# Four moves in the order of a two-layer kernel: a reading, a memset, a weight split and the parts of a tile

## The chip, the cores and the metric

The kernel runs on one core of a Trainium2 chip. The metric is device time in microseconds, the median of the runs shown. The profile is one further execution, recorded by the hardware profiler. The engines are called PE (TensorE, matmuls; PEld are its weight loads), DVE (VectorE), ACT (ScalarE), POOL (GpSimd) and SP (SyncE, which here only issues DMAs). Each runs its own instruction stream in a fixed order and waits on semaphores for the others.

## The reference

Four layers run over x of 2048 tokens x 640 features, in the order A, B, A, B, both A layers with the same weights and both B layers too. H is 32 heads of 20. Each layer adds its result to x.

```python
def _A_ref(x, wqkv, wo):            # x is layer-normed
    q, k, v = qkv[0], qkv[1], qkv[2]
    phi = lambda t: jnp.where(t > 0, t + 1, jnp.exp(t)) + 1e-6
    pq, pk = phi(q), phi(k)
    kv = jnp.einsum("bhsd,bhse->bhde", pk, v)
    z = jnp.einsum("bhsd->bhd", pk)
    num = jnp.einsum("bhqd,bhde->bhqe", pq, kv)
    den = jnp.einsum("bhqd,bhd->bhq", pq, z)[..., None] + 1e-6
    return (num / den) @ wo         # heads merged first
```

Layer B is causal softmax attention inside four segments of 512 tokens, mixed by a gate with a linear-attention memory that is carried from segment to segment, and a last product with its own `wo`. Only its weights and the key stacks of its attention matter here.

## The kernel before

**Staging.** A segment is 512 tokens, four tiles of 128. Matrices are split into two f16 halves, a rounded one and its rest, and a product is made of three f16 products; so 640 features are 5 blocks times 3, 15 matmuls for a tile and 320 columns ("a half").

**Layer A by algebra.** Values are never formed. Over the four segments the kernel sums G, the product of the normed x (its split form `xs`) with phi of the keys (`pk`), 640 x 640, in `g_first`: for each tile two key halves (`keys`), two query halves (`queries`, written to DRAM as `pqd`), and for each segment ten product chains of G (`memory`, L546 to L565, 12 matmuls each, summed on DVE at L562 or L564). In the first segment of the first layer all keys come first, then G, then the queries. In the last segment `merge` (L588) takes over: it sums the key column sums over all rows (L609) into `zb` and its scaled reciprocal `rz` (L610 to L612), takes the last chains of G, and forms from each block of G a "part": `eps` (L624), the scaled block `ge` (L626), its f16 copy on ACT (L628) and its rest on DVE (L629), five parts for each half of the columns. Then PE multiplies them with the value weight (L642), DVE and ACT cut the result to the heads (`kt`, L646 to L654), and PE multiplies with `wo` (L674, L679) into one matrix `wm`.

**The second half of layer A.** `p_read` (L694) reads a finished tile of queries: a DMA on SP (L698), a multiply with `zb` on POOL (L699), a sum for each head on DVE (L702), two small steps (L703, L704) and a second multiply on POOL (L705). `a_head` (L710) waits in the program for `L["zb"]`, reads three tiles and, once `wm` is there, turns the first. `a_second` (L721) reads the fourth, loads the residual rows `xo`, turns each tile (`turn`, L312: PE transposes, an ACT copy, a DVE subtraction), multiplies with `wm` (`o_half`), adds, and norms the result for layer B (`xh`).

**Weights.** `w_prep` (L228) loads a weight through the pool `stage` (two buffers), pauses `wait` pulls, takes the largest magnitude (DVE L240, L245; PE L248; DVE L250), pauses again, broadcasts it (PE L254), forms the scale, splits five blocks (ACT L264, DVE L265) and stores the split to DRAM (SP L270). With `behind` the reductions L240 are queued behind the last DVE subtraction of `turn`. `opening` (L1062) decides when each weight is prepared. Key weight first; `parts` (L475) makes `xs` from a normed tile (a copy on ACT, a subtraction on POOL).

**Side streams.** `weave(main, aux, per)` (L98) draws one piece of the main stream and then `per` pulls of the side stream; a pull is one step up to the next `yield`. In the opening's first segment `per` is 3, otherwise 2. `turns` alternates between two streams, `pause(n)` is n empty pulls. In the last segment the side stream prepares the key weight and the output weight of B and then runs `a_head`.

**The attention's pool.** `open_b` (L755) opens it in place of `stage` when the opening is over: three key stacks `ks`, whose rows 60, 61, 124 and 125 have to hold a constant. A memset fills the tile `one` (L760) and six DMAs on SP copy it (L763).

**What sets the order.** PE runs in the order in which the program writes its instructions. DVE, ACT, POOL and SP get theirs from a list scheduler that works through estimated times: of the instructions ready on an engine it takes the one written first, and a later one where none of those is ready. Instructions in a `high_priority` block go ahead of those outside. `issue_after(ins)` puts each instruction that its block writes on the engine of `ins` behind `ins` on that engine. The order is fixed before the run.

Of the kernel before, what the change touches and what calls it, by code (L numbers as in the profile page):

```python
# [14 lines left out]
OP = mybir.AluOpType  # L15
# [112 lines left out]
def pause(n):  # L128
    for _ in range(n):
        yield 0.0  # L130
# [12 lines left out]
class Kernel:  # L143
# [444 lines left out]
    def merge(self, L, wv, wo, memory, fill):  # L588
# [17 lines left out]
        for n in range(2):  # L606
# [6 lines left out]
            yield 4 * HN * COL  # L613
        L["zb"] = zb
        gs, eps = [], sb.tile([P, C], F32, tag="rca", name="eps", bufs=3)
        for n in range(2):
# [4 lines left out]
            for c in range(C):  # L621
                e = sb.tile([P, SEG], F32, tag="pq", name="ge", bufs=PQ)[:, :HN]
                if n == 0:
                    nc.vector.tensor_scalar(eps[:, c:c + 1], L["G"][c][:, HN:HN + 1], self.k_scl, 1e-6,  # L624
                                            op0=OP.mult, op1=OP.mult)
                nc.vector.scalar_tensor_tensor(e, L["G"][c][:, n * (HN + 1):n * (HN + 1) + HN], eps[:, c:c + 1],  # L626
                                               rz[:, n * HN:(n + 1) * HN], op0=OP.add, op1=OP.mult)
                nc.scalar.activation(t[:, c, 0, :HN], e, AF.Copy)  # L628
                nc.vector.tensor_tensor(t[:, c, 1, :HN], e, t[:, c, 0, :HN], op=OP.subtract)  # L629
        for _ in memory:  # L630
# [63 lines left out]
    def p_read(self, L, s, i, o):  # L694
# [3 lines left out]
        self.q_pqi.dma_start(pq, L["pqd"][s][i])  # L698
        nc.gpsimd.tensor_tensor(pq, pq, L["zb"][:, :D], op=OP.mult)  # L699
        q3 = pq.rearrange("p (h e) -> p h e", e=DH)  # L700
# [54 lines left out]
    def open_b(self):  # L755
        self.bp = self.ctx.enter_context(self.tc.tile_pool(name="attn", bufs=1))
        nc = self.nc
        self.ks = [self.bp.tile([P, 2, SEG], F16, name=f"ks{j}") for j in range(3)]
# [303 lines left out]
    def opening(self, src, stage, L, box):  # L1062
# [3 lines left out]
        def prep(key, keep=True):  # L1066
            w = self.w_tile(key) if keep else stage.tile([P, C, 2, D], F16, tag="split", name="split", bufs=1)
            if keep:
                self.w[key] = w
            yield from self.w_prep(key, stage, w, 0 if key == ("A", "k") else 3, key == ("A", "q"))  # L1070

# [39 lines left out]
        def others():  # L1111
            self.parts(first, cur[2], 0)
            for i in range(1, NT):
                xh = self.normed(*m[i - 1])
                yield from self.turn(xh, cur[1], i)
                self.parts(xh, cur[2], i)

        o = others()
        self.ones_columns()
        for s in range(NSEG):  # L1120
            nxt = []
            if s == 0:
                aux = chain(islice(o, 2), turns(o, a("q")), self.norms(src, 1, nxt, 6))
            elif s == 1:
# [149 lines left out]
```

## Time and profile before

| | |
|---|---|
| median of 3 runs | 1750.34 us (1749.05 to 1750.95) |
| the profiled execution | 1753.38 us |
| its span, first to last instruction | 1751.6 us |
| mean granted TensorE clock | 0.989 |
| instructions | 36286 |
| ACT, POOL busy | 994.8 us (57%), 541.2 us (31%) |

The span is what the profiler saw between the first and the last instruction; the time of the execution is 1.8 us longer. A row of a timeline gives start, length, engine, line, operation, output and inputs, shape and count of a group of like instructions, and in brackets how long the engine was idle before it and what ended that. The granted clock is the share of full speed that TensorE was allowed. Layer A of the first pair takes the first 300 us or so: the opening to 230, the merge to 275, then the second half, which runs on beside layer B. The second A layer sums G up to 1085 and merges up to 1128.

### The profile page before, as it was taken

How to read it: one execution, taken by the hardware profiler on the slowest of the kernel's cores; microseconds unless marked ns; L12 is line 12 of the kernel's file. 1: busy time of each engine (PE TensorE's matmuls, PEld its weight loads, DVE VectorE, ACT ScalarE, POOL GpSimd, SP SyncE). 2: the span in 40 equal slices, each digit the busy share in tenths (PEclk: the TensorE clock that was granted, in tenths of full speed). 3: DMA queues.
4: the chain of work that ended last, by engine and by line, in shares of the span. 5: the costliest groups of instructions: out<-in, count | busy, mean ns of one | idle time of the engine just before them, and what ended most of it. 6: DMA issues, size and time to landing. Idle time of an engine off the chain costs nothing.

```text
span 1751.6 us, 36286 instructions
## 1 busy us (share of the span) xinstructions
PE 1658.7 (95%) x13032; PEld 1034.7 (59%) x13032; DVE 1252.5 (72%) x3966; ACT 994.8 (57%) x1883; POOL 541.2 (31%) x1059
## 2 busy tenths in 40 slices
PE   5999988999999999999999999999999999999998
PEld 3677655564465456556656777666546545645555
DVE  7878685378787768768874465846778777878773
ACT  5666433346646655766676463333675576676673
POOL 3542131214213342333352210220422432333452
PEclk9999989999999999999999999999999999999999
DMA  5324535331321242344211303423232323323432
GB/s 212 143 83 154 207 147 204 104 118 54 98 93 58 90 133 73 106 146 133 81 54 39 114 31 121 158 97 129 66 105 83 107 77 110 102 81 111 137 107 91
DMA packets 110365, 190.89 MB, mean 109 GB/s; under 512 B 14172, under 2 KB 69596, under 8 KB 107624
## 3 DMA queue, kind: packets, MB, share of 16 engines
q1 hardware_dynamic: 97704, 142.68, 24.8%
q0 software_dynamic: 3264, 24.91, 4.0%
q10 hardware_dynamic: 9216, 20.98, 3.1%
q8 instruction: 103, 1.69, 0.4%
q14 instruction: 78, 0.64, 0.1%
HBM read 109.32 MB, written 78.64 MB: 107 GB/s over the span
## 4 chain that ended last, share of the span: by engine, by line
PE 71%; DVE 12%; ACT 7%; DMA 4%; POOL 3%; issue 2%; SPq 1%; ACTq 0%; POOLq 0%; DVEq 0%
PE ps L395 30%; PE ps L381 13%; PE ps L988 7%; PE ps L557 4%; PE ps L961 4%; PE ps L920 3%; PE ps L319 3%; ACT pe L965 3%; PE ps L446 2%; DVE ps L926 2%; PE ps L805 2%; PE ps L1001 1%; DMA pqi<-pqd 1%; DVE split L265 1%; DMA stage<-in_B_wo 1%
## 5 line engine op out<-in xcount | busy, mean ns | idle before, releaser
L926 DVE CUSTOM_DVE_ANT_0 ps<-ps,maskw 128x384 f32<-128x384 f32 (+3 forms) x1024 | 472.7, 518 | 41.3 <-PE ps L920 38.6
L965 ACT ACTIVATE pe<-ps,lsc 128x512 f32<-128x512 f32 x640 | 395.8, 697 | 76.1 <-PE ps L961 74.8
L395 PEld LDWEIGHTS <-xT 128*128 128x128 f16 x2880 | 283.4, 99 | 119.2 <-issue 9.8
L972 POOL TENSOR_SCALAR_AFFINE_SELECT pe<-pe 128x256 f32<-128x256 f32 (+1 forms) x640 | 229.6, 366 | 371.0 <-ACT pe L965 364.2
L395 PEld LDWEIGHTS <-oT 128*128 128x128 f16 x1920 | 186.4, 99 | 85.0 <-issue 5.9
L988 PE MATMUL ps<-pe,v 128*32 128x512 f32 (+3 forms) x2048 | 164.3, 436 | 12.5 <-POOL pe L972 7.2
L395 PE MATMUL ps<-w_Ak,xT 128*128 128x320 f16 x960 | 144.0, 307 | 3.7 <-DVE w_Ak L265 2.2
L395 PE MATMUL ps<-wm,oT 128*128 128x320 f16 x960 | 144.2, 303 | 3.2 <-ACT oT L323 1.6
L395 PE MATMUL ps<-w_Bo,oT 128*128 128x320 f16 x960 | 142.8, 301 | 1.6 <-ACT oT L323 0.7
L381 PE MATMUL ps<-xT,w_Bq 128*128 128x512 f16 x600 | 140.3, 379 | 2.8 <-ACT r L419 1.6
L926 DVE DVE_READ_ACCUMULATOR2_ANT mg<- 128x1 f32 x1024 | 142.7, 139 | 0.0
L395 PE MATMUL ps<-w_Bv,xT 128*128 128x320 f16 x960 | 141.1, 301 | 1.2 <-DVE otok L1008 1.2
L381 PE MATMUL ps<-xT,w_Bk 128*128 128x512 f16 x600 | 139.7, 382 | 1.2 <-ACT pe L965 1.2
L395 PE MATMUL ps<-w_Aq,xT 128*128 128x320 f16 x960 | 139.6, 302 | 1.1 <-DVE xT L324 1.0
L557 PE MATMUL ps<-pk,xs 128*128 128x321 f16 (+1 forms) x960 | 137.4, 300 | 2.3 <-DVE pk L531 1.8
L920 PE MATMUL ps<-ks,qs 60*128 60x512 f16 (+3 forms) x1024 | 123.2, 298 | 6.8 <-ACT pe L965 3.1
L557 PEld LDWEIGHTS <-xs 128*128 128x128 f16 x960 | 93.0, 97 | 39.8 <-issue 3.9
L770 DVE SCALAR_TENSOR_TENSOR nat<-ps,nat 128x512 f16<-128x512 f32 x80 | 55.1, 689 | 82.4 <-ACT nat L769 82.2
L988 PEld LDWEIGHTS ps<-pe,v 128*32 128x32 f32 x2048 | 65.4, 109 | 74.4 <-issue 39.6
L961 PE MATMUL ps<-qs,ks 62*128 62x512 f16 (+3 forms) x1024 | 106.6, 300 | 2.3 <-ACT pe L965 1.1
L410 DVE SCALAR_TENSOR_TENSOR e<-e,r 128x320 f32<-128x320 f32 x128 | 64.7, 505 | 56.5 <-ACT r L409 55.6
L769 ACT ACTIVATE nat<-ps 128x512 f16<-128x512 f32 x80 | 48.3, 604 | 88.3 <-PE ps L381 72.0
(197 smaller groups left out, 2424.3 us busy)
## 6 DMA issues: line engine op xcount, KB each, us to landing
x<-xn ACTq DMA_DIRECT2D x48, 320.0 KB
qs<-qd SPq DMA_DIRECT2D x128, 120.0 KB
ks<-kd SPq DMA_DIRECT2D x128, 120.0 KB
xo<-x SPq DMA_DIRECT2D x48, 320.0 KB
pqi<-pqd SPq DMA_DIRECT2D x32, 320.0 KB
qd<-nat SPq DMA_DIRECT2D x40, 256.0 KB
kd<-nat SPq DMA_DIRECT2D x40, 256.0 KB
x<-in_A_x SPq DMA_DIRECT2D x16, 320.0 KB
```

The costliest lines, as they stand in the source:

```text
L319: nc.tensor.transpose(pt[:, (c - c0) * P:(c - c0 + 1) * P], src[:, c * P:(c + 1) * P], self.ident)
L381: nc.tensor.matmul(p, w[:, c, a, t * P:(t + 1) * P], xT[:, c, b, :], start=k == 0, stop=k == 3 * C - 1)
L395: nc.tensor.matmul(p, xT[:, c, a, i * P:(i + 1) * P], w[:, c, b, n * HN:(n + 1) * HN], start=k == 0, stop=k == 3 * C - 1)
L410: nc.vector.scalar_tensor_tensor(e, e, 1.0, r, op0=OP.min, op1=OP.add)
L557: nc.tensor.matmul(p, xs[:, i, a, c * P:(c + 1) * P], pk[i][:, b, cols], start=k == 0, stop=k == 3 * NT - 1)
L770: nc.vector.scalar_tensor_tensor(nat[:, 1], p, QK_SHIFT, nat[:, 0], op0=OP.mult, op1=OP.subtract)
L920: nc.tensor.matmul(bs[par][:, a:a + n], qs[r, p, i * P:(i + 1) * P], ks[r, p, :n], start=True, stop=True)
L926: nc.vector.tensor_tensor_reduce(bs[par][:, a:a + n], bs[par][:, a:a + n], self.maskw[:, SEG - n:], 1.0, NEG, OP.add, OP.max, G["mg"][:, p ...
L961: nc.tensor.matmul(b[:, a:a + n], ks[r, p, j * P:(j + 1) * P], qs[r, p, j * P:], start=True, stop=True)
L965: nc.scalar.activation(e, b, AF.Exp, scale=self.lsc)
L972: nc.gpsimd.affine_select(d, d, pattern=pat, compare_op=OP.is_ge, fill=0.0, base=0, channel_multiplier=-1)
L988: nc.tensor.matmul(G["pv"][32 * h4:32 * h4 + 32, j * P:], v[j][:, h * E1:h * E1 + 32], G.pop((p, par, j)), start=j == 0, stop=j == 2, skip ...
```

## The change

Four moves. In `merge`, `L["zb"]` is set behind both halves of the parts of G instead of ahead of them, so that `a_head` writes its readings later, and the last part's DVE subtraction is kept as `L["split"]`; in `p_read` the first multiply is put in an `issue_after` block that names it. The memset of `one` and the six DMAs move to `open_stacks`, called with high priority. The pauses of `w_prep` become 0 for the query weight of A (3 before) and 6 for the output weight of B (3 before). In the first segment the side stream turns the three remaining tiles first, makes the parts of all four behind them, and then pulls the query weight's preparation: three pulls, 14 empty ones, the rest, and then the next segment's norms; before, the parts stood between the turns, and the preparation alternated with the turns.

```diff
--- before.py
+++ after.py
@@ -611,7 +611,6 @@
             nc.vector.reciprocal(rz[:, c], zb[:, c])
             nc.vector.tensor_scalar(rz[:, c], rz[:, c], self.k_inv, G_ONE, op0=OP.mult, op1=OP.mult)
             yield 4 * HN * COL
-        L["zb"] = zb
         gs, eps = [], sb.tile([P, C], F32, tag="rca", name="eps", bufs=3)
         for n in range(2):
             for _ in range(C - 2 if n == 0 else C):
@@ -626,7 +625,8 @@
                 nc.vector.scalar_tensor_tensor(e, L["G"][c][:, n * (HN + 1):n * (HN + 1) + HN], eps[:, c:c + 1],
                                                rz[:, n * HN:(n + 1) * HN], op0=OP.add, op1=OP.mult)
                 nc.scalar.activation(t[:, c, 0, :HN], e, AF.Copy)
-                nc.vector.tensor_tensor(t[:, c, 1, :HN], e, t[:, c, 0, :HN], op=OP.subtract)
+                L["split"] = nc.vector.tensor_tensor(t[:, c, 1, :HN], e, t[:, c, 0, :HN], op=OP.subtract)
+        L["zb"] = zb
         for _ in memory:
             pass
         yield from filled(1)
@@ -696,7 +696,8 @@
         nc = self.nc
         pq = self.row("pqi")
         self.q_pqi.dma_start(pq, L["pqd"][s][i])
-        nc.gpsimd.tensor_tensor(pq, pq, L["zb"][:, :D], op=OP.mult)
+        with self.tc.issue_after(L["split"].ins):
+            nc.gpsimd.tensor_tensor(pq, pq, L["zb"][:, :D], op=OP.mult)
         q3 = pq.rearrange("p (h e) -> p h e", e=DH)
         rc = self.sb.tile([P, H], F32, tag="rca", name="rca", bufs=3)
         nc.vector.tensor_reduce(rc, q3, axis=AX.X, op=OP.add)
@@ -754,6 +755,10 @@
 
     def open_b(self):
         self.bp = self.ctx.enter_context(self.tc.tile_pool(name="attn", bufs=1))
+        with self.tc.high_priority():
+            self.open_stacks()
+
+    def open_stacks(self):
         nc = self.nc
         self.ks = [self.bp.tile([P, 2, SEG], F16, name=f"ks{j}") for j in range(3)]
         one = self.bp.tile([P, 2, SEG], F16, tag="nat", name="one", bufs=2)
@@ -1067,7 +1072,8 @@
             w = self.w_tile(key) if keep else stage.tile([P, C, 2, D], F16, tag="split", name="split", bufs=1)
             if keep:
                 self.w[key] = w
-            yield from self.w_prep(key, stage, w, 0 if key == ("A", "k") else 3, key == ("A", "q"))
+            yield from self.w_prep(key, stage, w, 0 if key[0] == "A" and keep else 6 if key == ("B", "o") else 3,
+                                   key == ("A", "q"))
 
         def a(n):
             if n not in preps:
@@ -1109,18 +1115,20 @@
         with self.tc.issue_after(self.last.ins):
             m += [self.moments(x[i]) for i in range(2, NT)]
         def others():
-            self.parts(first, cur[2], 0)
+            xh = [first]
             for i in range(1, NT):
-                xh = self.normed(*m[i - 1])
-                yield from self.turn(xh, cur[1], i)
-                self.parts(xh, cur[2], i)
+                xh.append(self.normed(*m[i - 1]))
+                yield from self.turn(xh[i], cur[1], i)
+            for i in range(NT):
+                self.parts(xh[i], cur[2], i)
 
         o = others()
         self.ones_columns()
         for s in range(NSEG):
             nxt = []
             if s == 0:
-                aux = chain(islice(o, 2), turns(o, a("q")), self.norms(src, 1, nxt, 6))
+                q = a("q")
+                aux = chain(o, islice(q, 3), pause(14), q, self.norms(src, 1, nxt, 6))
             elif s == 1:
                 aux = chain(self.norms(src, 2, nxt, 6), a("v"), a("o"), late())
             elif s == 2:
```

## The prediction

> **What bounds it now.** I read the page's busy shares first, then the busy time of every engine in chosen stretches, then TensorE's timeline where a stretch has idle time, and then VectorE, GpSimd and the SP queue at those places.
>
> ```profile
> span 1751.6 us, 36286 instructions
> ## 1 busy us (share of the span) xinstructions
> PE 1658.7 (95%) x13032; PEld 1034.7 (59%) x13032; DVE 1252.5 (72%) x3966; ACT 994.8 (57%) x1883; POOL 541.2 (31%) x1059
> ```
>
> PE is busy for 1658.7 of 1751.6 us; 93 us are idle. Its order is written by hand and is otherwise back to back, so an idle microsecond on it is a microsecond of the end. The stretches (columns: stretch, length, busy time of PE, PEld, DVE, ACT, POOL, granted clock, DMA share, GB/s):
>
> ```profile
> 35.00:48.00 13.00, 9.36 (x49) 5.64 (x48) 10.08 (x34) 7.18 (x13) 4.74 (x7) 0.74 0.00 1
> 48.00:70.00 22.00, 19.68 (x148) 14.55 (x146) 21.55 (x49) 13.78 (x25) 10.29 (x13) 1.00 0.57 210
> 195.00:230.00 35.00, 30.71 (x213) 21.36 (x212) 23.57 (x53) 19.60 (x40) 10.18 (x14) 0.95 0.60 223
> 230.00:275.00 45.00, 37.15 (x303) 24.08 (x301) 39.61 (x86) 14.81 (x34) 11.90 (x15) 0.89 0.42 159
> 275.00:300.00 25.00, 19.59 (x123) 13.21 (x124) 10.18 (x27) 5.86 (x13) 4.41 (x5) 0.86 0.45 161
> 1085.00:1128.00 43.00, 39.72 (x334) 25.87 (x332) 36.95 (x83) 12.98 (x31) 10.36 (x13) 1.00 0.43 159
> ```
>
> Idle time of PE by length less busy time: 3.6 us in 35 to 48 (opening), 2.3 in 48 to 70 (first G), 4.3 in 195 to 230, 7.9 in 230 to 275 (merge of the first layer), 5.4 in 275 to 300 (its second half), 3.3 in the second merge: 27 of the 93. Where PE idled longest it also ran slower, at 0.74, 0.89 and 0.86. The change touches all of these but 195 to 230.
>
> **Part 1, the opening.** The transposition of the query weight's maximum (L248) and its broadcast (L254) stand among the key products.
>
> ```profile
> 30.98 4.24 PE L395 MATMUL ps<-w_Ak,xT 128*128 128x320 f16 x30
> 38.87 0.37 PE L248 MATMUL ps<-ident,wm 128*1 128x128 f32 x1 [3.64 <-DVE mv L340]
> 39.03 4.21 PE L395 MATMUL ps<-w_Ak,xT 128*128 128x320 f16 x15
> ```
>
> ```profile
> 52.27 2.08 PE L557 MATMUL ps<-pk,xs 128*128 128x321 f16 x14 [1.78 <-DVE pk L531]
> ```
>
> PE waits 3.64 us for the maximum and then takes 4.21 us for 15 products, where 30 took 4.24 before. In pulls of the side stream, three to each piece of the main one: before, L248 is the 13th pull, behind the fifth key half, and L254 the 17th, behind the sixth. After the change six pulls turn the tiles, three load and reduce, 14 pause; L248 is the 24th, behind the eighth and last half, L254 the 25th, behind the first product chain of G, and the five splits follow under the first two chains.
>
> So the three key halves left at 35.2 us run on at 2.1 each, to 41.5. What the last key tile needs of VectorE, from its groups between 29 and 57 us:
>
> ```profile
> L240 DVE TENSOR_REDUCE wmx<-stage 128x1 f32<-128x640 f32 x7 | 5.5, 806 | 0.0
> L265 DVE SCALAR_TENSOR_TENSOR w_Aq<-stage,scl_Aq,w_Aq 128x640 f16<-128x640 f32 x5 | 5.4, 1096 | 0.0
> L531 DVE SCALAR_TENSOR_TENSOR pk<-e,k_scl,pk 128x320 f16<-128x320 f32 x7 | 5.2, 742 | 0.0
> L338 DVE BATCH_NORM_STATS2 st<-x 128x6 f32<-128x320 f32 x8 | 3.6, 463 | 0.0
> L410 DVE SCALAR_TENSOR_TENSOR e<-e,r 128x320 f32<-128x320 f32 x7 | 3.3, 474 | 2.7 <-ACT r L409 2.7
> L324 DVE TENSOR_TENSOR xT<-ps,xT 128x256 f16<-128x256 f32 (+1 forms) x3 | 1.3, 458 | 0.0
> ```
>
> L531 5.2, L410 3.3, five L240 4.0 and L324 1.3 are 13.8 us from 29.4, so 43.2; and behind the last half's end come L410, L531 and three activations (taken at 0.5 each), 2.7, so 44.2. The later of the two rules, and the first chain of G ends at about 44.7 instead of 54.35 (52.27 + 2.08): 9.6 us at most. Part of it goes back: the moments of the next segment (3.6, and small steps that I put at half of that) now come behind the keys, and with the query splits (5.4) they make 10.8 us on VectorE, while PE takes some 7 us over four chains (12 products each, at the 2.08 for 14) up to the first turn that needs them; the other tiles' turns come 2 us apart. I let PE wait 3 there. **Gain 6.5, bounds 1 and 9.6**; the lower one holds if all 10.8 us are waited for less a chain's 2 (9.6 less 8.8). The copies and subtractions of the tile parts, moved behind the turns, are hidden by ACT's and POOL's free time ahead of G (7.18 and 4.74 busy of 13); without that cover a tile's part costs about what a key tile's tail does, 0.5 each, 2.
>
> **Part 2, the merge of the first layer.** PE waits ahead of L642 for the first part of G, while POOL and VectorE read the first three tiles of the segment.
>
> ```profile
> 244.50 2.20 PE L395 MATMUL ps<-w_Aq,xT 128*128 128x320 f16 x15
> 251.78 0.27 PE L642 MATMUL ps<-xT,w_Av 128*128 128x140 f16 x1 [5.08 <-ACT xT L628]
> ```
>
> ```profile
> 242.59 4.54 POOL L699 TENSOR_TENSOR pqi<-pqi,zb 128x640 f32<-128x640 f32 x3 [11.23 <-DMA pqi<-pqd]
> 248.38 3.97 POOL L705 TENSOR_TENSOR pqi<-pqi,rca 128x640 f32<-128x640 f32 x3 [1.26 <-DVE rca L703]
> ```
>
> ```profile
> L702 DVE TENSOR_REDUCE rca<-pqi x3: 819/820/821, 244.2 to 247.2; 128x32 f32<-128x640 f32 x3
> L703 DVE TENSOR_SCALAR rca<-rca x3: 117/168/769, 246.4 to 248.2; 128x32 f32<-128x32 f32 x3
> L704 DVE RECIPROCAL rca<-rca x3: 295/343/343, 247.9 to 248.9; 128x32 f32<-128x32 f32 x3
> ```
>
> ```profile
> L626 DVE SCALAR_TENSOR_TENSOR ge<-v,eps,rz x3: 539/1289/1554, 249.9 to 253.2; 128x320 f32<-128x320 f32 x3
> ```
>
> From 244.2 to 249.2 VectorE works on the reading or waits for it (three L702 at 0.82, the steps L703 and L704, the waits between), 5 us; then two of the first three L626 take 1.29 and 1.55 instead of 0.54, beside POOL's second multiplies: 1.8 us more. The change publishes `zb` only behind both halves of the parts, so this work is written behind all ten of them, and w_Bo's split behind the two sums. But VectorE is nearly full in this stretch (39.6 of 45), and two tiles' reading still stands ahead of the key tiles `kt` that come next. What is really gained is the idle part of those 5 us (5 less 2.5 of L702, 1.0 of L703, 1.0 of L704: 0.5), the third tile's reading, written behind the first `kt` (1.3), the 1.8, and 1 of the rest in places where VectorE waits anyway: 4.6, less 0.6 for whatever POOL now slows elsewhere. **Gain 4, bounds -1 and 6.8** (5 and 1.8; below nothing if POOL's first multiplies, 1.5 each, meet the parts and slow two of them as they slowed L626, with nothing gained).
>
> The tie itself does nothing: it orders instructions on the engine of the one it names, that one is the VectorE subtraction, and the multiply it encloses is on POOL. What acts is the later place in the program.
>
> Apart from the sum: the Trainium skill ("SBUF — State Buffer", Who interferes with whom) has it that a VectorE instruction with two SBUF inputs contends with a GpSimd instruction that reads SBUF, and that the first to start blocks the other for its whole length. The 1.29 and 1.55 beside the 0.54 agree. It speaks against this change: by it the three untied L699 could cost the parts their whole 4.54 us, and part 2 would come to nothing.
>
> **Part 3, the ones of the key stacks.**
>
> ```profile
> 235.32 0.33 SPq L270 DMA_DIRECT2D wd_Bo<-w_Bo  x1
> 235.83 2.64 SPq L698 DMA_DIRECT2D pqi<-pqd  x3
> 273.97 3.73 SPq L763 DMA_DIRECT2D ks<-one  x6
> 277.87 0.34 SPq L698 DMA_DIRECT2D pqi<-pqd  x1
> ```
>
> ```profile
> 273.03 0.91 DVE L760 MEMSET one<- 2x1024 f16 x1
> ```
>
> ```profile
> 289.03 0.55 PE L319 MATMUL ps<-ident,pqi 128*128 128x128 f32 x3 [3.61 <-POOL pqi L705]
> 291.19 4.24 PE L395 MATMUL ps<-wm,oT 128*128 128x320 f16 x15 [1.62 <-ACT oT L323]
> ```
>
> Six small writes wait on SP for a memset that VectorE does late, at 273; the fourth tile's reading and the residual rows queue behind them, and PE waits 3.61 and 1.62 us and then runs slow. The second layer has no such writes. The turns of the two layers, first layer first:
>
> ```profile
> L319 PE MATMUL ps<-ident,pqi x20: 272/273/421, 274.9 to 295.4; 128*128 128x128 f32 x20
> L319 PE MATMUL ps<-ident,xh x5: 272/272/273, 298.5 to 298.9; 128*128 128x128 f32 x5
> ```
>
> ```profile
> L319 PE MATMUL ps<-ident,pqi x20: 272/273/327, 1127.5 to 1140.9; 128*128 128x128 f32 x20
> L319 PE MATMUL ps<-ident,xh x5: 272/273/273, 1143.1 to 1143.5; 128*128 128x128 f32 x5
> ```
>
> From the first turn to the first of `xh` the first layer takes 23.6 us (274.9 to 298.5), the second 15.6. With priority the memset and the writes come once the stage is free, soon after w_Bo's store (235.32, some us later now), and the first layer goes like the second. **Gain 8, bounds 0 and 8.** The memset goes into a fuller stretch of VectorE (-0.5, bounds -0.9 and 0). The six writes (3.73 on SP) may stand ahead of the three readings, whose first use comes 39 us behind their issue: hidden, 3.7 without that.
>
> **Part 4, the second merge.** The same move; PE idles 3.3 us in that stretch. **Gain 2, bounds -1 and 3.3.** The output weight's longer pauses move two small products and five splits a few pieces on; the 4.3 us of 195 to 230 I leave (0, bounds -1 and 4.3).
>
> **Sum.** 6.5 + 4 + 8 - 0.5 + 2 = 20. The profiled execution took 1753.4 us (span 1751.6), so 1733.4; the median shown is 3 lower, so **1730.5**.
>
> **Rivals.** (a) The merges give nothing: the reading's work is only shifted to the key tiles, or POOL meets the parts. For it: VectorE is full. Then 6.5 + 8 - 0.5 stay: 1736.5; with both lower bounds 1738.5. (b) The opening gives back: PE waits at the turns and the queries instead. For it: VectorE is at 21.55 of 22 under the first G. With 1 in place of 6.5: 1736; with (a) too, 1742. (c) Slower: the orders of VectorE, ACT, POOL and SP come from estimated times, and a list dealt anew from the opening on may fall worse in the attention of the two B layers, 32 groups each. That is one place with one price: a few tenths of idle time of PE per group. It decides from 20 / 64 = 0.31 us per group; at 0.4 the time is 1756. For it: of PE's idle 93 us, 66 lie outside the six stretches above, so a group's share is at most 1 us now, in short waits. Against it: PE's order and the instructions there are the same. (d) It doesn't do what it says: the writes move ahead of the readings on SP, but the memset stays at 273, or nothing moves. The readings would issue at 277.7 and need 6.8 us to POOL (235.83 to 242.59), 1.5, 1.3 and 1.3, so that the first turn comes at 288.6 instead of 274.9; with 15.6 and 3 for the next two tiles `xh` is turned at 307, 8.7 later than now, and parts 1 and 4 give 8.5 back: 1750. It decides once the memset begins later than 256 (first turn at 270.9 less 10.9 and the writes' 3.7). Against it: the priority holds for the memset too, and its space is free long before.
>
> **Chances.** Forecast 0.55 (1725 to 1735), (a) and (b) 0.27, (c) 0.12, (d) 0.06. The range reaches over (a) and (b): 1722 to 1745. A measurement of this kernel tells about 0.2%, 3.5 us, from no change. Faster 0.82, within it 0.06, slower 0.12.
>
> **What would show it.** Part 1: no L248 between key halves and the first G chain ending near 45. Part 2: the wait ahead of the first L642 under 3 us, and L702 behind the last part. Part 3: memset and writes before 256, no wait for `pqi` at the fourth turn, some 16 us from the first turn to `xh`. Part 4: no wait at L642. Wrong would be a wait of PE of over 3 us at the turns before 70, or at the first turn of a layer.

## The result, and the profile after

The changed kernel takes **1736.61 us** in the median of 4 runs (1734.88 to 1737.10), the kernel before 1750.64 beside it (1749.05 to 1752.43): a ratio of 0.9918, 95% interval 0.9901 to 0.9935, a gain of 14 us. The prediction was 1730.5 with a range of 1722 to 1745: 6 us too low, inside the range, though outside the 1725 to 1735 of the forecast itself. The profiled execution of the changed kernel took 1736.56 us, with a span of 1734.8, where the one before had 1751.6.

Where the 16.8 us of the two spans lie is read from TensorE's timeline, by the starts of a few rows that both kernels have: the first query product of the opening (L395 on `w_Aq`), the sums' product (L609), the first turn of a read tile (L319 on `pqi`) and the first turn of `xh`. Some lines have other numbers in the changed kernel: L626 to L629 are L625 to L628 there, L699 to L705 are L700 to L706, and L760 and L763 are L765 and L768; rows of each run have that run's numbers.

| stretch | before | after | gain | predicted |
|---|---|---|---|---|
| start to first query product (part 1) | 69.48 | 64.34 | 5.1 | 6.5 |
| to the sums of the first layer | 160.83 | 161.84 | -1.0 | 0 |
| first merge, sums to first turn (part 2) | 44.57 | 45.34 | **-0.8** | 4 |
| first turn to `xh` (part 3) | 23.62 | 15.54 | 8.1 | 7.5 |
| to the sums of the second pair of layers | 790.62 | 789.49 | 1.1 | 0 |
| second merge (part 4) | 38.40 | 37.05 | 1.4 | 2 |
| first turn to `xh` | 15.54 | 15.56 | 0.0 | 0 |
| rest | 608.54 | 605.64 | 2.9 | 0 |

The last 2.9 is no work of the change: TensorE's waits in that stretch are the same to a tenth of a microsecond, group by group, but for one of 0.6 that only the kernel before has, and over all the runs below the stretch takes 604.3 to 608.6; I put it down to the clock that happens to be granted (0.989 in the mean of the whole execution before, 0.992 after). So the account is 5 for the opening, 8 for the stacks, and next to nothing for the two merges.

The opening, TensorE's timeline after the change (start, length, instruction, count, idle time ahead of it and what ended it):

```profile
28.95 12.39 PE L395 MATMUL ps<-w_Ak,xT 128*128 128x320 f16 x90
41.17 0.27 PE L248 MATMUL ps<-ident,wm 128*1 128x128 f32 x1
...
45.10 0.43 PE L557 MATMUL ps<-pk,xs 128*128 128x321 f16 x2 [1.39 <-DVE pk L531]
45.46 0.40 PE L254 MATMUL ps<-wm,ones 1*128 1x1 f32 x2
45.79 8.35 PE L557 MATMUL ps<-pk,xs 128*128 128x321 f16 x48
```

Six key halves now stand in one unbroken row of 90 products, L248 is behind it and waits for nothing, and the first chain of G ends at 45.5. But the 48 products behind it take 8.35 us. The granted clock there, in the view by stretches (length, busy time and count of PE, PEld, DVE, ACT, POOL, clock, DMA share, GB/s):

```profile
46.00:54.00 8.00, 8.00 (x49) 5.29 (x48) 7.45 (x18) 6.17 (x9) 5.89 (x7) 0.81 0.01 3
```

The stacks' ones, on the SP queue, on VectorE, and in the turns:

```profile
239.33 4.55 SPq L768 DMA_DIRECT2D ks<-one  x6
244.04 0.84 SPq L698 DMA_DIRECT2D pqi<-pqd  x2
```

```profile
238.39 0.91 DVE L765 MEMSET one<- 2x1024 f16 x1 [0.15 <-DVE v L564]
```

```profile
L319 PE MATMUL ps<-ident,pqi x20: 272/273/328, 271.5 to 284.9; 128*128 128x128 f32 x20
L319 PE MATMUL ps<-ident,xh x5: 272/272/273, 287.1 to 287.5; 128*128 128x128 f32 x5
```

The memset is at 238, not 273, the writes follow at once, and the last read tile is turned at 284.9 and `xh` at 287.1, with no wait between. That is part 3 as predicted.

The first merge is the part that failed. The same groups of TensorE in it, before (230.31 to 274.88) and after (226.18 to 271.52): line, shape and count, busy time and mean, idle time ahead of them.

```profile
L642 PE MATMUL ps<-xT,w_Av 128*128 128x140 f16 (+1 forms) x90 | 7.6, 246 | 7.9 <-ACT xT L628 5.7 <-DVE xT L629 2.1
L679 PE MATMUL ps<-w_Ak,kt 128*32 128x320 f16 x48 | 6.2, 303 | 0.0
L674 PE MATMUL ps<-w_Ak,kt 128*128 128x320 f16 x30 | 5.8, 302 | 0.0
```

```profile
L679 PE MATMUL ps<-w_Ak,kt 128*32 128x320 f16 x48 | 7.4, 344 | 0.1
L674 PE MATMUL ps<-w_Ak,kt 128*128 128x320 f16 x30 | 7.1, 346 | 4.6 <-DVE kt L654 3.7 <-ACT kt L653 0.9
L642 PE MATMUL ps<-xT,w_Av 128*128 128x140 f16 (+1 forms) x90 | 6.2, 216 | 2.7 <-DVE xT L628 1.4 <-ACT xT L627 0.9
```

The wait at the value weight's products (L642) went from 7.9 to 2.7, as it should. In its place stand 4.6 us at the next products, those with the key tiles (L674), and 2.5 us by which those and L679 run slower (7.4 and 7.1 against 6.2 and 5.8). TensorE's timeline shows the one large wait, and VectorE's and GpSimd's show what it was for:

```profile
254.59 0.45 PE L674 MATMUL ps<-w_Ak,kt 128*128 128x320 f16 x2 [0.95 <-ACT kt L653]
258.71 0.45 PE L674 MATMUL ps<-w_Ak,kt 128*128 128x320 f16 x1 [3.67 <-DVE kt L654]
```

```profile
254.65 4.01 DVE L654 TENSOR_TENSOR kt<-ke,kt 128x140 f16<-128x140 f32 x1
...
259.33 0.23 DVE L654 TENSOR_TENSOR kt<-ke,kt 128x140 f16<-128x140 f32 x1
```

```profile
230.15 3.11 POOL L700 TENSOR_TENSOR pqi<-pqi,zb 128x640 f32<-128x640 f32 x2 [3.77 <-DVE zb L610]
...
253.85 1.28 POOL L706 TENSOR_TENSOR pqi<-pqi,rca 128x640 f32<-128x640 f32 x1
255.06 0.17 POOL L194 MEMSET v<- 128x32 f32 x1
255.12 0.58 POOL L276 DMA_DIRECT2D w_Bq<-wd_Bq  x1
255.72 1.28 POOL L706 TENSOR_TENSOR pqi<-pqi,rca 128x640 f32<-128x640 f32 x1
256.95 1.53 POOL L700 TENSOR_TENSOR pqi<-pqi,zb 128x640 f32<-128x640 f32 x1
```

The granted clock behind that wait, by stretches:

```profile
259.00:264.00 5.00, 4.88 (x20) 1.48 (x20) 3.10 (x9) 1.37 (x5) 0.60 (x1) 0.50 0.45 186
```

One subtraction of a key tile, 128 by 140, takes 4.01 us where its like takes 0.23. It begins while GpSimd multiplies and ends at 258.66, 0.2 us behind the last of three multiplies (258.48). These are the multiplies of the reading that the change was to keep out of the way. Two of the first multiplies (L700) already ran at 230, ahead of the parts: GpSimd was idle, and a later place in the program does not hold back an engine that has nothing else to do.

In the second merge the first key tile is held in the same way, for 2.65 us beside two multiplies (1097.71 to 1100.49), and TensorE waits 0.7 and 0.3 there. The largest new wait is of another kind (VectorE's timeline, then TensorE's and VectorE's again):

```profile
1098.00 2.65 DVE L654 TENSOR_TENSOR kt<-ke,kt 128x140 f16<-128x140 f32 x1
```

```profile
1108.23 0.31 PE L679 MATMUL ps<-w_Ak,kt 128*32 128x320 f16 x1 [2.19 <-DVE kt L654]
```

```profile
1107.06 0.82 DVE L703 TENSOR_REDUCE rca<-pqi 128x32 f32<-128x640 f32 x1 [2.48 <-POOL pqi L700]
1107.79 0.17 DVE L704 TENSOR_SCALAR rca<-rca 128x32 f32<-128x32 f32 x1
1107.88 0.29 DVE L654 TENSOR_TENSOR kt<-ke,kt 128x140 f16<-128x140 f32 x1
```

This subtraction, of the fourth key tile, takes 0.29 itself. It stands in VectorE's queue behind a reduction of the reading, which waits 2.48 us for a multiply.

### The profile page after: what moved, and what is told of

Same layout as the page of the kernel before. It is cut to its first block, busy times and chain, and to the rows that moved or that the text cites. A ratio compares the mean times of both kernels' runs of the same rounds, so it can differ in the third digit from the quotient of the medians.

```text
span 1734.8 us, 36293 instructions
## 1 busy us (share of the span) xinstructions
PE 1651.8 (95%) x13032; PEld 1031.2 (59%) x13032; DVE 1252.2 (72%) x3966; ACT 995.6 (57%) x1883; POOL 541.1 (31%) x1059
## 4 chain that ended last, share of the span: by engine, by line
PE 70%; DVE 13%; ACT 7%; DMA 4%; issue 3%; POOL 2%; SPq 1%; ACTq 0%; POOLq 0%; DVEq 0%
PE ps L395 28%; PE ps L381 13%; PE ps L993 7%; PE ps L557 4%; PE ps L966 4%; PE ps L925 3%; PE ps L319 3%; ACT pe L970 3%; PE ps L446 2%; DVE ps L931 2%; PE ps L810 2%; PE ps L1006 1%; DVE xn L472 1%; DVE split L265 1%; DVE st L338 1%
## 5 line engine op out<-in xcount | busy, mean ns | idle before, releaser
L395 PEld LDWEIGHTS <-xT 128*128 128x128 f16 x2880 | 282.4, 99 | 115.8 <-issue 8.6
L395 PEld LDWEIGHTS <-oT 128*128 128x128 f16 x1920 | 184.5, 98 | 81.6 <-issue 5.9
L395 PE MATMUL ps<-w_Ak,xT 128*128 128x320 f16 x960 | 141.1, 304 | 2.7 <-ACT w_Ak L264 1.5
L395 PE MATMUL ps<-wm,oT 128*128 128x320 f16 x960 | 141.7, 299 | 2.0
L395 PE MATMUL ps<-w_Bo,oT 128*128 128x320 f16 x960 | 141.2, 299 | 1.5 <-ACT oT L323 0.7
L395 PE MATMUL ps<-w_Aq,xT 128*128 128x320 f16 x960 | 140.5, 303 | 1.2 <-DVE xT L324 1.1
L395 PE MATMUL ps<-w_Bv,xT 128*128 128x320 f16 x960 | 139.7, 299 | 0.6 <-DVE otok L1013 0.6
L557 PEld LDWEIGHTS <-xs 128*128 128x128 f16 x960 | 93.6, 98 | 40.6 <-issue 2.1
L410 DVE SCALAR_TENSOR_TENSOR e<-e,r 128x320 f32<-128x320 f32 x128 | 65.2, 509 | 53.2 <-ACT r L409 52.3
```

Of the source, the lines that this page charges most:

```text
L395: nc.tensor.matmul(p, xT[:, c, a, i * P:(i + 1) * P], w[:, c, b, n * HN:(n + 1) * HN], start=k == 0, stop=k == 3 * C - 1)
L410: nc.vector.scalar_tensor_tensor(e, e, 1.0, r, op0=OP.min, op1=OP.add)
L557: nc.tensor.matmul(p, xs[:, i, a, c * P:(c + 1) * P], pk[i][:, b, cols], start=k == 0, stop=k == 3 * NT - 1)
```

## The experiments

The theories. PORT: a VectorE instruction with two operands in SBUF cannot run while GpSimd multiplies, so the move took the reading's multiplies off the parts and put them on the key tiles. ORDER: VectorE is simply full, and the work stands ahead of the key tiles whatever GpSimd does. TIE: the tie of the change is without effect (compiled without it, the program has the same instructions in the same order on every engine), and a tie that acts would give the gain. Of each run: the time, the ratio to the kernel before run beside it with its 95% interval, and the stretches of the profiled execution, read as in the table above.

| run | median us | ratio | opening | merge 1 | turns | merge 2 |
|---|---|---|---|---|---|---|
| before (profiled 1753.4) | 1750.64 | 1 | 69.5 | 44.6 | 23.6 | 38.4 |
| the change | 1736.61 | 0.9918 (0.9901 to 0.9935) | 64.3 | 45.3 | 15.5 | 37.1 |
| opening alone | 1746.61 | 0.9978 (0.9970 to 0.9987) | 65.3 | 44.8 | 23.9 | 38.3 |
| stacks alone | 1745.02 | 0.9969 (0.9957 to 0.9981) | 70.9 | 44.5 | 15.5 | 38.6 |
| move alone | 1750.05 | 0.9995 (0.9987 to 1.0004) | 69.1 | 44.1 | 22.9 | 36.9 |
| change, move undone | 1736.65 | 0.9916 (0.9903 to 0.9930) | 65.1 | 44.5 | 15.6 | 38.2 |
| no second multiply | 1736.48 | 0.9913 (0.9900 to 0.9927) | 62.9 | 41.9 | 15.6 | 40.9 |
| tie on the reduction | 1740.52 | 0.9937 (0.9924 to 0.9949) | 65.1 | 46.9 | 15.5 | 38.3 |
| reading behind the keys | 1737.51 | 0.9915 (0.9901 to 0.9928) | 64.1 | 42.2 | 16.2 | 40.6 |
| masked key in PSUM | 1736.41 | 0.9919 (0.9905 to 0.9932) | 63.1 | 44.8 | 15.5 | 37.6 |
| and third reading behind keys | 1732.55 | 0.9899 (0.9883 to 0.9914) | 63.7 | 43.7 | 15.5 | 34.4 |
| and reading in two steps | 1726.30 | 0.9863 (0.9848 to 0.9879) | 64.5 | 39.0 | 15.7 | 33.3 |
| two steps, key in SBUF | **1724.17** | 0.9844 (0.9829 to 0.9859) | 62.9 | 39.0 | 15.8 | 33.3 |
| two steps, sums early | 1725.19 | 0.9851 (0.9834 to 0.9867) | 62.7 | 38.9 | 15.7 | 33.3 |

**The parts one by one.** Three kernels take one part each of the change into the kernel before. The opening alone is the rewritten `others()`, the pause of 14 and the A weights without pauses:

```diff
-                aux = chain(islice(o, 2), turns(o, a("q")), self.norms(src, 1, nxt, 6))
+                q = a("q")
+                aux = chain(o, islice(q, 3), pause(14), q, self.norms(src, 1, nxt, 6))
...
-            yield from self.w_prep(key, stage, w, 0 if key == ("A", "k") else 3, key == ("A", "q"))
+            yield from self.w_prep(key, stage, w, 0 if key[0] == "A" and keep else 3, key == ("A", "q"))
```

> The kernel before with the opening alone (tiles turned first, parts behind, query weight's reduction after them, 14 pauses, pauses of the A weights to nothing). From the two traces the opening gave 5.1 us and took 1.0 back up to the first merge: 1746, within 1.5. My sum had 6.5: 1744. If a list dealt anew cost something further on (rival c) it would be seen here, as this part alone changes TensorE's order: 1748 or more.

Measured: 1746.6, 3.9 us less by the ratio (2.3 to 5.3), within what was expected and below the 1748 of rival (c), which the interval just reaches. The later stretches are as before.

```diff
+        with self.tc.high_priority():
+            self.open_stacks()
```

> The kernel before with the priority for the ones of the key stacks alone. By my sum 8 less 0.5: 1743; from the trace of the change 8.1 between the first turn and the turn of xh: 1742.5. If the fourth tile's reading was late for another reason than the writes ahead of it on SP, the gain needs the other parts too, and alone this gives 4 or less: 1746 or more.

Measured: 1745.0, or 5.4 us less (3.3 to 7.5), some 2 short of what was expected. At its place the whole 8.1 is there (23.6 to 15.5), so the late writes were the cause by themselves. Its profiled opening is 1.5 longer than before with the same order on TensorE; over the runs with the new opening that stretch varies as much, from 62.7 to 65.3.

```diff
-        L["zb"] = zb
         gs, eps = [], sb.tile([P, C], F32, tag="rca", name="eps", bufs=3)
...
+        L["zb"] = zb
         for _ in memory:
```

> The kernel before with the later publication of the sums alone, without the tie. By my sum 6 in both merges: 1744.5. Theory PORT: the waits ahead of the first product with the value weight go and as much returns at the key tiles: 1749.5 to 1751, and a key tile subtraction of over 2 us in each merge.

Measured: 1750.05, a ratio of 0.9995 whose interval holds 1. In the first merge one key tile subtraction took 3.35 us and TensorE waited 3.02 for it, as in the whole change; the merge was 0.5 us shorter. In the second merge one took 2.65, as in the whole change, and the merge gains 1.5. The parts alone add up to 10.2 us by their ratios, the change to 14.4; the intervals of the sum (3 us to each side) and of the change (3 also) meet. The opening and the stacks alone add up to 9.3 (2.6 to each side), and the change without the move, which comes next, gains 14.7 (2.4 to each side); these just fail to meet. Whether the parts help one another, or the longer pauses of B's output weight, which no run takes alone, gain something, is open.

**The move taken out of the change.** The other side of the same question: publication ahead of the parts again, all else as changed.

```diff
+        L["zb"] = zb
         gs, eps = [], sb.tile([P, C], F32, tag="rca", name="eps", bufs=3)
...
-        L["zb"] = zb
         for _ in memory:
```

> The changed kernel with one part of the change taken back: the sums are published ahead of the parts again, in both merges, and the tie that goes with it is gone. My sum priced the move at 6 us in both merges (4 and 2): then this one takes about 1742.6. Theory PORT (the reading's GpSimd multiplies now hold the subtraction of the key tiles as they held the parts before, so the move is worth 1.35 less 0.8, from the two traces): 1737, within 1.5, with the wait ahead of the first product with the value weight back at about 5 us, and no wait of 3 us at the key tiles.

Measured: 1736.65. The move is worth nothing that can be measured; the 6 us of the sum were not in it. TensorE's wait is back at the value weight, somewhat shorter than expected (its timeline in the first merge):

```profile
245.87 0.28 PE L642 MATMUL ps<-xT,w_Av 128*128 128x140 f16 x1 [3.68 <-ACT xT L628]
```

**What holds the key tile: without the second multiplies.**

```diff
-        nc.gpsimd.tensor_tensor(q3, q3, rc[:, :, None].to_broadcast([P, H, DH]), op=OP.mult)
+        if not lone:
+            nc.gpsimd.tensor_tensor(q3, q3, rc[:, :, None].to_broadcast([P, H, DH]), op=OP.mult)
```

> The changed kernel without the second GpSimd multiply of the first three tiles read in each segment (the sums that normalise them are left out, so the output differs). In the first merge two of these multiplies and a first one, 4.1 us in a row, lay over the one key tile subtraction that took 4.01 us where the others take 0.25. Theory PORT: the subtraction falls to below 1.8 us, the wait of 3.67 at the key tile goes with it, and the first merge from its sums to the first turn falls from 45.3 to 42 or less; the kernel to about 1732. Theory ORDER (VectorE is simply full: the reading's reductions stand ahead of the key tiles, whatever GpSimd does): the wait at the key tiles stays at 2.5 us or more and the merge at 44.5 or more; about 1736.

VectorE and GpSimd in the first merge:

```profile
252.62 1.57 DVE L654 TENSOR_TENSOR kt<-ke,kt 128x140 f16<-128x140 f32 x1
```

```profile
252.48 1.55 POOL L700 TENSOR_TENSOR pqi<-pqi,zb 128x640 f32<-128x640 f32 x1
```

With two multiplies gone the subtraction takes 1.57, to 254.19, again 0.16 behind the end of the one multiply that is left (254.03). The first merge falls to 41.9, as PORT has it and against ORDER: VectorE still had the same reductions in front. The kernel's time did not follow, a miss: 1736.5. The second merge lost 3.8, since there a reduction now waits 4.79 us in VectorE's queue, as in the 2.48 above, and TensorE 4.42 behind it. So there are two ways in which the reading gets at the key tiles, and both have to go.

**A tie that acts.**

```diff
-        with self.tc.issue_after(L["split"].ins):
-            nc.gpsimd.tensor_tensor(pq, pq, L["zb"][:, :D], op=OP.mult)
+        nc.gpsimd.tensor_tensor(pq, pq, L["zb"][:, :D], op=OP.mult)
...
-        nc.vector.tensor_reduce(rc, q3, axis=AX.X, op=OP.add)
+        with self.tc.issue_after(L["split"].ins):
+            nc.vector.tensor_reduce(rc, q3, axis=AX.X, op=OP.add)
```

> The changed kernel with the tie put where it acts: on the VectorE reduction of the reading, behind the last subtraction of the parts, in place of the GpSimd multiply. Theory TIE (part 2 failed because the tie of the change is without effect, and what it was meant to order gives the 4 us): the first merge falls from 45.3 to about 41.5, the kernel to 1732. Theory PORT: the multiplies only start 1 to 2 us later and meet the key tiles just as well: one key tile subtraction of 2.5 us or more stays in the first merge, 1736 within 1.5.

Measured: 1740.5, if anything slower than the change (ratios 0.9937 and 0.9918, whose intervals overlap). TIE falls: all three reductions now come behind the last part, and their three multiplies fall on the second key tile (VectorE's and GpSimd's timelines of the first merge). One first multiply, which no tie holds, also met the parts: an L625 took 1.99 us, and TensorE waited 2.17 at the value weight.

```profile
258.05 3.33 DVE L654 TENSOR_TENSOR kt<-ke,kt 128x140 f16<-128x140 f32 x1
```

```profile
257.47 3.73 POOL L706 TENSOR_TENSOR pqi<-pqi,rca 128x640 f32<-128x640 f32 x3
```

**The reading wholly behind the key tiles.**

```diff
-        L["zb"] = zb
         for _ in memory:
...
+        L["zb"] = zb
         for v in L["v"]:
             self.ones_column(v)
```

(The tie is on the reduction, as in the run before, and names the last key tile's subtraction.)

> The changed kernel with the sums published behind the five key tiles instead of behind the parts, and the reading's reduction tied behind the last key tile's subtraction. Theory PORT: no key tile subtraction over 0.6 us, no wait of TensorE at the key tiles over 1 us, and both merges gain: the first from 45.3 to about 41.5, the second from 37.05 to about 35; together 1731, provided the reading is ready at the first turn. Theory ORDER: the work only moves on once more, and is late at the first turn of the read tiles, with a wait there of 3 us or more: 1736 or more.

This missed too. The first merge was short (42.2), but not for the reason expected: one subtraction was held once more, now by the *first* multiplies, which no tie holds back and which ran as soon as their rows had landed (the same two timelines):

```profile
254.76 4.08 DVE L653 TENSOR_TENSOR kt<-ke,kt 128x160 f16<-128x160 f32 x1 [0.93 <-ACT kt L652]
```

```profile
254.14 4.51 POOL L699 TENSOR_TENSOR pqi<-pqi,zb 128x640 f32<-128x640 f32 x3
```

And in the second merge the reading is late: its rows are fetched behind the key tiles too, and TensorE waits 7.31 us at the first turn. ORDER's half is true of a reading that is put off as a whole.

**The operand alone.** The work and its times stay; the subtraction gets one operand in PSUM.

```diff
-            e = sb.tile([P, 512], F32, tag="er", name="ke", bufs=3)[:, :hi - lo]
+            e = p[:, :hi - lo]
```

> The changed kernel with one thing more: the masked key tile is written back over its own PSUM bank instead of into SBUF, so that the key tile's subtraction has one operand in SBUF and one in PSUM; nothing is left out and VectorE and GpSimd have the same work. Theory PORT in the form 'two SBUF operands on VectorE shut out by a GpSimd multiply': the subtraction takes under 0.6 us though the multiplies run over it, TensorE's wait of 3.67 goes and the slow products behind it, and the first merge falls from 45.3 to about 41.5; the second from 37.05 to about 36.3, since its wait of 2.19 is for a reduction that stands ahead in VectorE's queue. Kernel 1732. Rival PLACE (whatever VectorE does beside a GpSimd multiply is stretched): the subtraction still takes 2 us or more, merge 44 or more, 1736.5.

VectorE and GpSimd in the first merge:

```profile
253.36 0.24 DVE L654 TENSOR_TENSOR kt<-ps,kt 128x140 f16<-128x140 f32 x1
253.52 0.30 DVE L650 SCALAR_TENSOR_TENSOR ps<-ps,blk 128x140 f32<-128x140 f32 x1
253.73 3.75 DVE L410 SCALAR_TENSOR_TENSOR e<-e,r 128x320 f32<-128x320 f32 x1
257.40 0.29 DVE L654 TENSOR_TENSOR kt<-ps,kt 128x140 f16<-128x140 f32 x1
```

```profile
252.48 1.28 POOL L706 TENSOR_TENSOR pqi<-pqi,rca 128x640 f32<-128x640 f32 x1
...
254.36 1.28 POOL L706 TENSOR_TENSOR pqi<-pqi,rca 128x640 f32<-128x640 f32 x1
255.59 1.53 POOL L700 TENSOR_TENSOR pqi<-pqi,zb 128x640 f32<-128x640 f32 x1
```

This run decides the mechanism. Beside a multiply (252.48 to 253.76) the subtraction with one SBUF operand takes 0.24, and L650, with one in PSUM and one in SBUF, 0.30. The next instruction with both operands in SBUF, a step of phi of the queries (L410, 0.48 elsewhere), takes 3.75, to 257.48, behind the last multiply. PLACE falls. The time does not change (1736.4), for the hold only went to the next such instruction, with the next subtraction queued behind it; the expected 1732 was wrong because I had looked at one victim.

**Which half of the reading must move.** Two kernels on top of that one. The first writes the third tile's reading behind the key tiles, the second writes load and first multiply of all three behind the parts, and reductions and second multiplies behind the key tiles.

```diff
         for i in range(3):
+            while i == 2 and L.get("kt") is None:
+                yield 0.0
             yield from self.p_read(L, s, i, box["o"])
```

> As the run with the masked key in PSUM, and the third tile's reading is written behind the key tiles. Theory QUEUE (in the second merge the reduction of the third tile waits in VectorE's queue for its row and holds up the key tile behind it, 2.19 us): second merge about 35, first merge 41.5 as without this edit, kernel 1730. Rival LATE: the second tile's reduction takes the third's place in the queue, or the third tile is late at its turn, and the second merge stays at 36.5 or more: 1732 or more.

```diff
+        while L.get("kt") is None:
+            yield 0.0
         rc = self.sb.tile([P, H], F32, tag="rca", name="rca", bufs=3)
...
-        for i in range(3):
-            yield from self.p_read(L, s, i, box["o"])
+        reads = [self.p_read(L, s, i, box["o"]) for i in range(3)]
+        if L.get("kt") is None:
+            for r in reads:
+                next(r)
+        for r in reads:
+            yield from r
```

(`L["kt"] = kt` is set behind the loop over the key tiles in both, and the tie is left out of the second.)

> As the run with the masked key in PSUM, and the reading is written in two steps: load and first multiply of three tiles behind the parts, reductions and second multiplies behind the last key tile. Theory QUEUE: no reduction in front of a key tile, second merge 35, first merge 41; but the second multiplies come behind, and if they are late at the first turn TensorE waits there up to 1.5 us, as with the reading wholly behind the key tiles: 1730 to 1732. Rival LATE: wait of 3 us or more at the first turn of a layer: 1734 or more.

The first gives 1732.6: second merge 34.4 as QUEUE expects, first merge still 43.7, with a wait of 1.63 behind the same kind of hold. The second gives 1726.3: no multiply between 235.2 and 262.2, where parts and key tiles are made, and no reduction there before 259.8, when the last key tile's subtraction has begun; merges of 39.0 and 33.3, both shorter than expected, and waits of 0.9 and 1.3 behind the first turned tile.

**What of it is needed.** Two more kernels take one thing each out of the two-step kernel: the key in PSUM (first), and the later publication that is the change's own (second).

```diff
-            e = p[:, :hi - lo]
+            e = sb.tile([P, 512], F32, tag="er", name="ke", bufs=3)[:, :hi - lo]
```

> The kernel with the reading in two steps, with the masked key tile in SBUF again as in the changed kernel. In the two-step run no multiply of GpSimd ran between 235.2 and 262.2, where the key tiles are made, so the operand's place should not matter any more: 1726.5, first merge 39, second 33.3. Rival BOTH (the key in PSUM is worth something of its own, or its banks): 1729 or more, with a key tile subtraction of over 1 us.

```diff
+        L["zb"] = zb
         gs, eps = [], sb.tile([P, C], F32, tag="rca", name="eps", bufs=3)
...
-        L["zb"] = zb
         for _ in memory:
```

> The kernel with the reading in two steps (masked key in PSUM), with the sums published ahead of the parts as in the kernel before. If the change's later publication is beside the point, and only the place of the reductions and second multiplies counts: the three first multiplies run at the same time, 1726.3, merges 39 and 33.3. If the later publication has a worth of its own: the reading's first multiplies come among the parts, a wait ahead of the first product with the value weight of 1 us or more, 1728 or more.

1724.2 and 1725.2, with the same merges. The operand's place no longer matters, and neither does the place of the publication: the three first multiplies run at 228 in both. The first of the two is the fastest kernel here, by 0.75% ahead of the change (0.9844 against 0.9918, intervals apart) with a handful of lines; the intervals of the three two-step kernels meet. The key tiles' subtractions in its first merge (durations in ns, least, median, most), and TensorE's timeline in its second merge, which now has no wait at all from the sums to the first turn:

```profile
L654 DVE TENSOR_TENSOR kt<-ke,kt x5: 243/305/325, 251.9 to 257.8; 128x140 f16<-128x140 f32 x4, 128x160 f16<-128x160 f32 x1
```

```profile
1087.97 3.06 PE L642 MATMUL ps<-xT,w_Av 128*128 128x80 f16 x60
1090.87 0.57 PE L675 MATMUL ps<-w_Ak,kt 128*128 128x320 f16 x3
```

## Why the prediction was right in part, and where it failed

**Part 1** (6.5 predicted, 5.1 in the profiles, 3.9 for the part alone) had the right mechanism, and a size that came near by errors that cancel. Keys to 41.5: they ended at 41.3. First chain of G at 44.7: 45.5. But I set that against 54.35, which is the end of the *second* chain (10 and 14 products, 24 in all). Like against like, the 12th product ended at 52.70 before and ends at 45.53 now, so the gain there is 7.2 and not 9.6. The 3 us of waits at the turns did not come; the query splits and moments were hidden. What was lost instead is 2.0 between the 12th product and the 24th (54.35 before, 49.19 now), and most of that is clock (TensorE's timeline in the changed kernel, then without second multiplies):

```profile
45.79 3.40 PE L557 MATMUL ps<-pk,xs 128*128 128x321 f16 x12
```

```profile
45.34 1.82 PE L557 MATMUL ps<-pk,xs 128*128 128x321 f16 x12
```

The granted clock is 0.50 under the first row and 1.00 under the second, and the opening of the second run is 62.9. Of the eleven kernels with the new opening, the four whose clock is 1.00 from 43 to 53 us reach the first query product at 62.7 to 63.1, the other seven, at 0.66 to 0.83, at 63.7 to 65.3. So an execution without this loss gains about the 6.5 that I predicted, but not by my sum.

**Part 2** (4 predicted, -0.8 measured) failed in one term: "less 0.6 for whatever POOL now slows elsewhere". The first steps held, and gave more than the 4.6 of the sum: the waits at the value weight fell by 5.2, and its products ran 1.4 faster. But what GpSimd slowed elsewhere cost 4.7 of waits at the key tiles and 2.5 of slow products behind them. I had named the key tiles as next, as a full VectorE, in rival (a), and the Trainium skill's rule apart from the sum, and then priced the meeting at the parts alone. The shorthand "what acts is the later place in the program" was wrong for half of the work: two of the first multiplies ran at 230 in spite of it, and the first reduction at 249.93, ahead of the last two subtractions of the parts (250.65 to 251.53), where I had put it behind them.

The rule of the Trainium skill ("SBUF — State Buffer", Who interferes with whom), that a VectorE instruction with two SBUF inputs contends with a GpSimd instruction that reads SBUF and one with at most one, outside the modes that use both ports, does not, is borne out here: 4.01, 4.08, 3.33 and 3.75 us against 0.24 and 0.30. I had set it against the change, but with the parts as the victim.

**Part 4** (2 predicted, 1.4 measured): the wait at the value weight went, as predicted, and 3.2 came back at the key tiles, 1.0 of it at the first, whose subtraction was held, and 2.2 behind a reduction in VectorE's queue. "No wait at L642" was right, and not enough.

**Part 3** (8 less 0.5; 8.1) was right in each step: memset and writes before 256, no wait at the fourth tile, 15.5 us from the first turn to `xh`. The 0.5 for the memset did not show: with the stacks alone the first merge, where it now lies, takes 44.5, as before.

Rival (a), "the merges give nothing", came true, and it is because the range was drawn to reach over it that the time lies inside. That it meets the 1736.5 of (a) to 0.1 us is luck: the opening gave less than stands there, the stacks and the merges a little more. Rivals (b) and (c) did not come true: the opening alone gained, and the stretches with the B layers are no longer than before. The tie does nothing, as the prediction said.

The gain that part 2 was after does exist, and is larger than I allowed: 44.6 to 39.0 in the first merge and 38.4 to 33.3 in the second. In the second my upper bound was TensorE's idle time, 3.3; the other 1.9 is busy time, 35.1 against 33.3: the 90 products with the value weight cover 6.5 us before and 5.1 in the two-step kernel, at a mean of 216 and 217 ns, so broken up by waits they overlap less.

## What to carry to other kernels

A wait that goes from one consumer can turn up at the next one in line unless the work that caused it leaves the whole stretch; so before moving work, list every instruction in the stretch that the moved work can hold, by queue and by where its operands lie, and price the move at the next victim. A later place in the program holds nothing back on an idle engine: split the work at the point where it starts to hurt (here the reductions and second multiplies), and let the rest run early. An edge is real only if the compiled order differs with and without it.

## What the runs showed of the hardware that was not expected

Whether a held VectorE instruction is let in between multiplies differs from place to place. In the changed kernel GpSimd had 0.6 us between two of them (255.1 to 255.7, a memset of 0.17 and the issue of a transfer), and the subtraction, waiting since 254.65, still ended only behind the third. The PSUM run shows the same with L410. In the kernel before it was let in: of the two long L626, 249.94 to 251.23 and 251.15 to 252.70, each ended 0.35 us behind the end of a multiply (250.88 and 252.36), and the third multiply, from 250.84, took 1.52 where the two ahead of it took 1.27. What decides it, no run here tells.

TensorE's clock falls after less waiting than I had thought. In the run with the third reading behind the keys, three short waits stand close together (TensorE's timeline), and from within the third the clock is at half (the view by stretches; 1.00 from 255.5 to 256.1, 0.50 from 256.2 on):

```profile
253.63 0.73 PE L675 MATMUL ps<-w_Ak,kt 128*128 128x320 f16 x3 [0.96 <-ACT kt L653]
254.58 0.45 PE L680 MATMUL ps<-w_Ak,kt 128*32 128x320 f16 x2 [0.22 <-ACT kt L653]
256.65 0.45 PE L680 MATMUL ps<-w_Ak,kt 128*32 128x320 f16 x1 [1.63 <-DVE kt L654]
```

```profile
257.00:263.00 6.00, 6.00 (x27) 1.97 (x27) 3.02 (x9) 2.06 (x7) 2.14 (x2) 0.50 0.57 230
```

A single wait of 2.19 us in the second merge of the change was followed by no such fall (1.00 from 1108 to 1113). The Trainium skill ("TensorE: Matmul & The Clock Gate", HAM oscillation — how this bites in real kernels) puts the limit at one idle gap of about 3.4 us. The 3.67 of the first merge, with 0.50 behind it, seems to agree, but the clock was 1.00 from 257.0 to 257.3 and 0.50 from 257.4 on, some 2.3 us into that wait; the three short waits do not agree. The length of the waits alone does not decide: in the opening, waits of 1.19 and 1.39 us at the same two products go with a clock of 0.66 from 43 to 53 us in the run of the opening alone, and with 1.00 in the run with the masked key in PSUM. In all the traces here a stretch at half clock within the execution lasts 3.4 us, or two or three times that. No run was made to tell more.
